# Which queue carries the opening loads: strict order on SyncE, a table load first and two weight blocks on ScalarE

## The chip, the cores and the metric

One core of one Trainium2 chip. The metric is the device time of one launch in microseconds (us). TensorE is written PE, VectorE DVE, ScalarE ACT, GpSimd POOL and SyncE SP. "Landed" is when a transfer's completion semaphore is full. One program on one core has no second die to compare with.

## The reference, cut to what matters

```python
x = A_x                                   # 2048 x 640, bf16
xn = layernorm(x)
q, k, v = split(xn @ wqkv)                # 32 heads of 20
pq, pk = q @ w_phi, k @ w_phi             # per head
phi = concat(softmax(p), softmax(-p))     # feature map, for q and k
kv, z = sum over s of phi_k (x) v, phi_k
o = phi_q kv / (phi_q z + 1e-6)
return x + o @ wo + (silu(xn @ w1) * (xn @ w3)) @ w2
```

The opening concerns only the first 512 rows (four tiles of 128 rows, called rows 0 to 3 below), their normalisation, and v = xn @ wv for them. The matrix wv is loaded in five blocks of 128 x 640 (160 KB), and a row tile has 160 KB too.

## The kernel before

The loads of the opening, as issued:

```python
def load_wv(c, queue=nc.sync):
    queue.dma_start(out=wv[:, c, :], in_=wqkv3[:, c, 2 * D : 3 * D])

def setup():
    ...
    nc.vector.memset(xg[0][:, 0, 320:328], 0.0)
    nc.sync.dma_start(out=xg[0][:, 0, 0:320], in_=x2[0:P, 0:320])        # row 0, first half
    nc.scalar.dma_start(out=xg[0][:, 0, 320:640], in_=x2[0:P, 320:640])  # row 0, second half
    load_x(xg[0], 1, 1, 0)          # row 1
    load_wv(0, nc.scalar)
    load_wv(1)
    load_wv(2, nc.scalar)
    load_x(xg[0], 2, 1, 0)          # row 2
    load_wv(3, nc.scalar)
    load_wv(4)
    load_x(xg[0], 3, 1, 0)          # row 3
    load_gu(0)                      # first gate/up weights: 2 x 480 KB
    ...                             # wrow, load_gu(1), wkT (transposed), rows 4-7, load_gu(2), load_gu(3)

def warm():
    warm_ps.append(bank([P, 512], f32))
    dummies(8)                      # 8 matmuls of 512 columns on constants, the first work of TensorE
```

What uses them, in the order in which TensorE and VectorE take it (cut):

```python
plan.op("ACT", 1.3, lambda: nc.scalar.preload_act_table(AF.Sqrt), after=3.2)
ln_stats(0); c0 = center(0, 0, 256); ...          # VectorE: row 0
x0 = [T(0, ...)(), T(0, ...)()]                   # TensorE: transposes of row 0
ln_stats(1); c2 = center(1, 0, 640)
V_part(0, (0, 1), ...); V_part(0, (2,), ...)      # v of row 0, wv blocks 0, 1, 2
e2, e3 = T(1, ...)                                # transposes of row 1
vo[0]["last"] = V_part(0, (3, 4), ...)            # v of row 0, wv blocks 3, 4
...
ln_stats(2); ...; apply2 = ln_apply(2)
V_part(1, (0, 1), ...); V_part(1, (2, 3, 4), ...) # v of row 1, all five blocks
e2, e3 = T(2, ..., apply2)                        # transposes of row 2
...                                               # v of rows 2 and 3, then gate/up matmuls without pause
```

The softmax here doesn't subtract the row's maximum and nothing guards it: scores larger than these inputs give would overflow.

## Time and profile before

| | before |
|---|---|
| time | 269.59 us (median of 6; 269.18 to 270.17) |
| span of the profiled execution | 267.9 us |
| first gate/up matmul ("dense start" below) | 13.38 us |

From the page of the kernel before: span, busy time by engine, DMA queues (q1 is SyncE's, q10 ScalarE's: packets, MB, share of 16 engines), and the engines of the chain of work that ended last.

```profile
span 267.9 us, 5109 instructions
...
PE 262.6 (98%) x1948; PEld 165.1 (62%) x1974; DVE 173.8 (65%) x334; ACT 122.4 (46%) x273; POOL 131.5 (49%) x118
...
q1 hardware_dynamic: 68784, 37.18, 50.8%
q10 hardware_dynamic: 720, 0.61, 0.7%
...
PE 96%; DMA 2%; issue 1%; ACTq 0%; DVE 0%
```

The chain is TensorE nearly throughout. From 13.4 us on its gaps sum to 1.4 us. So a change to the opening can gain only by moving the moment at which this dense work starts.

TensorE's timeline of the kernel before, 3 to 15 us. Columns: start us, length us, engine, line, operation, out<-in, shape, count, and in brackets idle time ahead with what ended it.

```profile
4.21 0.73 PE L416 MATMUL bank<-ident,xn 128*128 128x128 bf16 x5
...
5.08 1.60 PE L461 MATMUL bank<-wv,xnT 128*128 128x320 bf16 x6
...
7.14 2.08 PE L461 MATMUL bank<-wv,xnT 128*128 128x320 bf16 x14 [0.17 <-DMA wv<-in_A_wqkv_dram]
9.12 0.73 PE L416 MATMUL bank<-ident,xn 128*128 128x128 bf16 x10
...
13.38 1.24 PE L667 MATMUL bank<-xnT,w_107 128*128 128x512 bf16 x4
```

L416 are the transposes, L461 the v matmuls, L667 gate/up. Six v matmuls take 1.60 us at 5.08 but fourteen take 2.08 us at 7.14: the same shape at half the rate, then at full rate.

VectorE's timeline of the kernel before: row 2's statistics and, 1.7 us later, its normalised tile.

```profile
6.92 0.89 DVE L297 BATCH_NORM_STATS2 stats<-xg 128x6 f32<-128x320 bf16 x2 [0.90 <-DMA xg<-in_A_x_dram]
...
8.61 0.45 DVE L352 TENSOR_SCALAR xn<-xg,mv,rstd 128x640 bf16<-128x640 bf16 x1
```

VectorE was idle for 0.90 us until row 2 landed (6.89 us); its tile is done at 9.06, and TensorE takes it at 9.12.

ScalarE's timeline of the kernel before, 0 to 6 us. ACTq is its sequencer issuing transfers.

```profile
0.96 0.38 ACTq L183 DMA_DIRECT2D xg<-in_A_x_dram  x1
1.36 1.42 ACTq L175 DMA_DIRECT2D wv<-in_A_wqkv_dram  x3
2.82 1.28 ACT L915 ACT_TABLE_LOAD   x1 [2.82 <-issue]
```

The windows 2:4, 4:6 and 6:8 us of the kernel before. The last two columns are the mean busy share of the DMA engines and GB/s.

```profile
2.00:4.00 2.00, 2.00 (x6) 0.59 (x4) 1.23 (x4) 1.18 (x1) 1.25 (x10) 1.00 0.99 280
4.00:6.00 2.00, 2.00 (x13) 1.27 (x13) 1.92 (x7) 1.20 (x4) 0.00 (x0) 1.00 1.03 309
6.00:8.00 2.00, 1.83 (x16) 1.19 (x15) 1.06 (x5) 0.75 (x2) 0.00 (x0) 1.00 1.00 305
```

The DMA engines are full all through the opening.

### The profile page before, as it was taken

The numbers are of one execution on the slowest core, as the hardware profiler recorded it, in microseconds if no ns is written. First come the engines' busy times: TensorE is split into PE (matmuls) and PEld (weight loads), VectorE is DVE, ScalarE is ACT, GpSimd is POOL, SyncE is SP. The second block draws the span as 40 slices with busy tenths as digits, with TensorE's granted clock in tenths as the row PEclk, the third lists the DMA queues.
The fourth block names the chain that finished last, engine by engine and source line by source line (L and its number), as shares of the span: only waits on it lengthen the run. The fifth ranks groups of instructions, "written<-read, shape, count | busy, mean of one in ns | idle before, by whom it ended". The sixth has DMA issues, their size and how long they took to land.

```text
span 267.9 us, 5109 instructions
## 1 busy us (share of the span) xinstructions
PE 262.6 (98%) x1948; PEld 165.1 (62%) x1974; DVE 173.8 (65%) x334; ACT 122.4 (46%) x273; POOL 131.5 (49%) x118
## 2 busy tenths in 40 slices
PE   8999999999999999999999999999999999999995
PEld 4645555555565666666555677765765665657774
DVE  4738798777665996876898748666367365443221
ACT  3857676656776676767545222234225213120000
POOL 3263679976557577699315715443542553111000
PEclk9999999999999999999999999999999999999999
DMA  7999949200420027529295457495913938430401
GB/s 210 310 264 300 265 128 298 74 0 0 134 64 0 2 98 202 115 108 148 77 292 179 130 144 201 150 258 183 220 38 119 234 112 210 123 82 20 124 25 49
DMA packets 69528, 38.10 MB, mean 142 GB/s; under 512 B 49664, under 2 KB 67456, under 8 KB 69504
## 3 DMA queue, kind: packets, MB, share of 16 engines
q1 hardware_dynamic: 68784, 37.18, 50.8%
q10 hardware_dynamic: 720, 0.61, 0.7%
q8 instruction: 15, 0.25, 0.4%
q14 instruction: 9, 0.07, 0.1%
HBM read 12.81 MB, written 12.98 MB: 96 GB/s over the span
## 4 chain that ended last, share of the span: by engine, by line
PE 96%; DMA 2%; issue 1%; ACTq 0%; DVE 0%
PE bank L667 38%; PE bank L447 22%; PE bank L832 19%; PE bank L845 8%; PE rtbank L742 2%; PE bank L461 2%; DMA wv<-in_A_wqkv_dram 2%; PE bank L620 1%; PE kva L592 1%; PE kvb L592 1%; PE bank L416 0%; ACTq L175 0%; ACTq L183 0%; DVE res L859 0%; DVE xg L181 0%
## 5 line engine op out<-in xcount | busy, mean ns | idle before, releaser
L711 POOL TENSOR_TENSOR hT<-gs,up 128x512 bf16<-128x512 bf16 x43 | 49.7, 1156 | 81.0 <-ACT up L706 41.8
L667 PE MATMUL bank<-xnT,w_108 128*128 128x512 bf16 x235 | 59.2, 379 | 0.3
L667 PE MATMUL bank<-xnT,w_107 128*128 128x512 bf16 x219 | 58.2, 379 | 1.1
L832 PE MATMUL bank<-w_109,hT 128*128 128x320 bf16 (+2 forms) x396 | 55.1, 295 | 0.0
L447 PEld LDWEIGHTS <-xnT 128*128 128x128 bf16 x440 | 42.1, 98 | 17.6
L832 PEld LDWEIGHTS <-hT 128*128 128x128 bf16 x396 | 37.9, 98 | 15.2
L683 ACT ACTIVATE th<-bank 128x512 bf16<-128x512 f32 x48 | 28.7, 597 | 39.8 <-PE bank L667 39.1
L688 DVE SCALAR_TENSOR_TENSOR gs<-th,bank 128x512 bf16<-128x512 bf16 x48 | 32.8, 684 | 20.6 <-ACT th L683 20.0
L667 PEld LDWEIGHTS <-w_108 128*128 128x128 bf16 x240 | 23.5, 98 | 28.3
L859 DVE TENSOR_TENSOR res<-bank,xr 128x320 bf16<-128x320 f32 (+2 forms) x33 | 15.8, 478 | 38.6 <-PE bank L845 38.6
L706 ACT ACTIVATE up<-bank 128x512 bf16<-128x512 f32 x43 | 25.7, 597 | 22.5 <-PE bank L667 22.5
L667 PEld LDWEIGHTS <-w_107 128*128 128x128 bf16 x240 | 22.4, 97 | 20.9
L845 PE MATMUL bank<-wo,oT 128*128 128x320 bf16 (+2 forms) x165 | 24.7, 295 | 0.0
L447 PE MATMUL bank<-wkphi,xnT 128*128 128x320 bf16 x160 | 24.3, 299 | 0.0
L447 PE MATMUL bank<-wqphi,xnT 128*128 128x320 bf16 x160 | 24.3, 299 | 0.0
L845 PEld LDWEIGHTS <-oT 128*128 128x128 bf16 x165 | 15.8, 98 | 5.8
L447 PE MATMUL bank<-wv,xnT 128*128 128x320 bf16 x120 | 18.3, 299 | 0.0
L519 ACT ACTIVATE exp_128<-bank 128x320 bf16<-128x320 f32 x32 | 11.5, 435 | 13.6 <-PE bank L447 13.6
L519 ACT ACTIVATE exp_131<-bank 128x320 bf16<-128x320 f32 x32 | 11.5, 437 | 12.2 <-PE bank L447 12.2
L519 ACT ACTIVATE exp_129<-bank 128x320 bf16<-128x320 f32 x32 | 11.5, 435 | 10.7 <-PE bank L447 10.7
L519 ACT ACTIVATE exp_130<-bank 128x320 bf16<-128x320 f32 x32 | 11.5, 439 | 10.1 <-PE bank L447 10.1
L297 DVE BATCH_NORM_STATS2 stats<-xg 128x6 f32<-128x320 bf16 x32 | 13.7, 470 | 2.7 <-DMA xg<-in_A_x_dram 2.7
(141 smaller groups left out, 294.5 us busy)
## 6 DMA issues: line engine op xcount, KB each, us to landing
xr<-in_A_x_dram SPq DMA_DIRECT2D x4, 640.0 KB, 5.4
out_dram<-res SPq DMA_DIRECT2D x15, 160.0 KB, 1.9
w_107<-in_B_w_dram SPq DMA_DIRECT2D x4, 480.0 KB, 6.5
w_108<-in_B_w_dram SPq DMA_DIRECT2D x4, 480.0 KB, 6.8
w_109<-in_B_w_dram SPq DMA_DIRECT2D x1, 1920.0 KB, 8.7
xg<-in_A_x_dram SPq DMA_DIRECT2D x11, 160.0 KB, 3.7
wo<-in_A_wo_dram SPq DMA_DIRECT2D x1, 800.0 KB, 5.1
xg<-in_A_x_dram SPq DMA_DIRECT2D x1, 640.0 KB, 5.1
```

Source lines behind the costliest of these rows:

```text
L297: nc.vector.bn_stats(out=stats[:, t, h, :], in_=xg[c][:, i, h * 320 : (h + 1) * 320])
L447: nc.tensor.matmul(o["ps"][:], xnT[:, c, t * P : (t + 1) * P], w[:, c, 320 * half : 320 * half + 320], start=(c == 0), stop=(c == KD - 1),)
L461: nc.tensor.matmul(o[half]["ps"][:], xnT[:, c, t * P : (t + 1) * P], wv[:, c, 320 * half : 320 * half + 320], start=(c == 0), stop=(c == K ...
L519: nc.scalar.activation(out=box["e"][:, sgn, 16 * half : 16 * half + 16, :], in_=o["ps"][:].rearrange("p (h d) -> p h d", d=Dh), func=AF.Ex ...
L667: nc.tensor.matmul(o["ps"][:], w[:, k, fi * P : (fi + 1) * P], xs[:, k, :], start=(k == 0), stop=(k == KD - 1))
L683: nc.scalar.activation(out=box["th"][:], in_=og["ps"][:], func=AF.Tanh, scale=0.5)
L688: nc.vector.scalar_tensor_tensor(out=box["gs"][:], in0=box["th"][:], scalar=1.0, in1=og["ps"][:], op0=ALU.add, op1=ALU.mult)
L706: nc.scalar.activation(out=box["up"][:], in_=ou["ps"][:], func=AF.Copy, scale=0.5)
L711: lambda: nc.gpsimd.tensor_mul(out=hT[c][:, fi, :], in0=box["gs"][:], in1=box["up"][:]),
L832: nc.tensor.matmul(o["ps"][:], hT[c][:, fi, ti * P : (ti + 1) * P], w2[:, fi, lo:hi], start=(fi == 0), stop=False,)
L845: nc.tensor.matmul(o["ps"][:], oT[c][:, k, ti * P : (ti + 1) * P], wo_of[0][:, k, lo:hi], start=False, stop=(k == KD - 1),)
L859: nc.vector.tensor_tensor(out=box["res"][:, lo:hi], in0=o["ps"][:], in1=xr[c][:, ti, lo:hi], op=ALU.add)
```

## The change

Its intent: land the opening tiles in the order of their use by sending them down one queue, get the activation table out of the way first, and let ScalarE carry only two blocks that are used late. Rows 8 to 13 are also loaded in pairs.

```diff
         nc.vector.memset(xg[0][:, 0, 320:328], 0.0)
+        nc.scalar.preload_act_table(AF.Sqrt)
         nc.sync.dma_start(out=xg[0][:, 0, 0:320], in_=x2[0:P, 0:320])
-        nc.scalar.dma_start(out=xg[0][:, 0, 320:640], in_=x2[0:P, 320:640])
+        nc.sync.dma_start(out=xg[0][:, 0, 320:640], in_=x2[0:P, 320:640])
         load_x(xg[0], 1, 1, 0)
-        load_wv(0, nc.scalar)
+        load_wv(0)
         load_wv(1)
-        load_wv(2, nc.scalar)
+        load_wv(2)
+        load_wv(3, nc.scalar)
         load_x(xg[0], 2, 1, 0)
-        load_wv(3, nc.scalar)
-        load_wv(4)
+        load_wv(4, nc.scalar)
         load_x(xg[0], 3, 1, 0)
 ...
-        X_of[t] = plan.op("SP", 0.5, lambda: [load_x(xg[c], i, 1, c)], ...)
+        n = 2 if t < 14 else 1
+        if i % n == 0:
+            X_of[t] = plan.op("SP", 0.5, lambda: [load_x(xg[c], i, n, c)], ...)
+        else:
+            X_of[t] = X_of[t - 1]
 ...
-    plan.op("ACT", 1.3, lambda: nc.scalar.preload_act_table(AF.Sqrt), after=3.2)
```

More of the change, by code (lines that the diff above doesn't have):

```diff
@@ L403, in fetch @@
             xg_of[c] = plan.alloc("five", al)
-        X_of[t] = plan.op("SP", 0.5, lambda: [load_x(xg[c], i, 1, c)], deps=[xg_of[c]], lat=2.5, after=30.0)
+        n = 2 if t < 14 else 1
+        if i % n == 0:
+            X_of[t] = plan.op("SP", 0.5, lambda: [load_x(xg[c], i, n, c)], deps=[xg_of[c]], lat=2.5, after=30.0)
+        else:
+            X_of[t] = X_of[t - 1]
         ln_stats(t, ("k", k))
```

## The prediction

> **What bounds the kernel now.** TensorE. The page gives PE 98% busy; the chain that ended last is 96% PE. After 13.4 us the PE idle gaps in the trace sum to only 1.4 us of 254, none over 0.06 us, so nothing changed there can gain. The one DMA piece on the chain is in the opening: 4.77 us for a wv load that ended at 7.10 us. So the question is when the dense gate/up work (13.38 us on the timeline) can start.
>
> **The opening before.** x and wv are nine 160 KB blocks (one split in halves), issued on two queues, about 0.46 us an issue. They land: row 0 at 2.68/2.89, row 1 3.81, wv0 4.99, wv1 5.21, wv2 5.57, row 2 6.89, wv3 7.10, wv4 7.39, row 3 7.82. The DMA engines are full from 2 to 14 us (DMA share about 1.0, 270 to 325 GB/s). The page total is fixed, so the change can only reorder. TensorE then is never far from its feeder: it idles about 0.2 to 0.3 us for wv3 at 7.14; row 2's transposes at 9.12 follow VectorE's normalised row (9.06), which follows the landing of row 2 (VectorE idled 0.90 us for it, timeline); small waits for ScalarE/VectorE copies at 9.87 and 11.9.
>
> **What the change does.**
> 1. Takes three issues and half of row 0 from ScalarE to SyncE. Row 0's second half is issued 0.3 us later (1.25 instead of 0.96) but shares less; I expect it at about 2.9 to 3.1. First statistics and transposes: within 0.15 us of before.
> 2. The table load (1.28 us, at 2.82 before, followed by 0.56 us of ScalarE idle) was off the chain. Moving it gains nothing directly.
> 3. The Trainium skill, "Perfetto Trace Analysis", "DVE / Act Engine Instruction", says that the sequencer pushes an instruction and goes on to decode the next. The trace agrees for VectorE (a semaphore instruction at 2.92 inside a statistics instruction of 2.71 to 3.20). So I expect wv3's issue by 1.0 us, beside the table load, not behind it (65%); otherwise at 2.1. wv4 waits for a recycled semaphore (row 0's first half, about 2.7). So "late" blocks come early and share bandwidth with rows 0, 1 and wv0/wv1: wv3 lands near 4.0, wv4 near 6.0, wv1 5.2 to 5.9, wv2 5.5 to 6.2, row 2 6.6 to 7.2, row 3 7.2 to 7.8. (Estimate: the slowest engine's rate, 1.47 MB by 7.82 us, some 0.27 MB/us.)
> 4. The wv3 wait of 0.3 us goes, but wv1/wv2 may cost TensorE some of it, and row 2's chain moves by -0.3 to +0.3 us.
> 5. Rows 8 to 13 in pairs: eight issues become five. They were at 27 to 31 us on SyncE; no VectorE wait for them shows, and the transposed group 1 lands at 42.7 while its first use is at 49.5. No effect. The planner's order of VectorE/ScalarE work may shift slightly, within slack.
>
> **Sum.** Opening ends -0.5 to +0.3 us from before, best -0.15; the rest carries it unchanged. Predicted 269.4 us, 8 in 10 between 268.6 and 270.1. Faster by over 2%: 0.01; within 2%: 0.985; slower: 0.005.
>
> **What would show it.** Right: PE busy time unchanged; first gate/up matmul at 12.9 to 13.7; no wait for wv3/wv4; the time difference equals the shift of that matmul; wkT still lands near 18.7 before its use. Wrong on 3: wv3's issue after the table load's end. Wrong on 5: a PE or VectorE wait over 0.3 us after 25 us.
>
> **What would make it wrong.** Strict order letting row 2 land before 6.5 (gain to 1 us); a planner reorder starving TensorE; another moment of the clock's warm-up (matmuls were slow until 6.5 us).

## The result, and the profile after

| | before | after |
|---|---|---|
| median of the same rounds | 269.44 us (20 runs) | 270.14 us (10 runs; 269.75 to 271.06) |
| ratio of the fast runs | | 1.0031, 95% interval 1.0019 to 1.0044 |
| profiled execution | 269.57 us | 271.37 us |
| first gate/up matmul | 13.38 us | 13.99 us |

A ratio is the mean time of one kernel's fast runs over that of the other's fast runs of the same rounds, so it is not quite the ratio of the medians. The change is a small loss, some 0.8 us. The runs of the changed kernel fall in two clusters, six at 269.75 to 270.32 and four at 270.77 to 271.06. The profiled execution is slower than any of them, so it must not be taken for a typical one.

When each opening transfer landed, in us, worked out from the completion records of the two traces:

```
          row0a row0b row1  wv0   wv1   wv2   row2  wv3   wv4   row3  w1[0]  w3[0]  wkT    rows4-7
before    2.68  2.89  3.81  4.99  5.21  5.57  6.89  7.10  7.39  7.82   9.56  11.32  18.70  20.31
after     3.21  3.90  5.62  6.04  6.46  7.10  7.51  3.38  4.19  7.90  12.02  13.45  20.74  23.38
```

From the page of the changed kernel:

```profile
span 269.7 us, 5106 instructions
...
PE 262.5 (97%) x1948; PEld 164.6 (61%) x1974; DVE 173.9 (64%) x334; ACT 122.5 (45%) x273; POOL 131.6 (49%) x118
...
q1 hardware_dynamic: 69024, 37.42, 50.8%
q10 hardware_dynamic: 432, 0.36, 0.4%
...
PE 89%; SPq 5%; DMA 3%; issue 1%; DVE 1%
```

TensorE does the same work in the same busy time, but transfers and SyncE's issuing now take 8% of the chain, where transfers took 2% before. ScalarE's timeline of the changed kernel shows what its two "late" blocks did:

```profile
0.79 1.28 ACT L182 ACT_TABLE_LOAD   x1 [0.79 <-PEq L1098]
0.82 0.87 ACTq L175 DMA_DIRECT2D wv<-in_A_wqkv_dram  x2
```

They are issued at 0.82 and 1.24 us, beside the table load and before SyncE's second transfer. They land first of all weights (3.38 and 4.19). VectorE's timeline of the changed kernel: rows 0, 1 and 2 are waited for in turn.

```profile
3.23 0.49 DVE L298 BATCH_NORM_STATS2 stats<-xg 128x6 f32<-128x320 bf16 x1 [2.30 <-DMA xg<-in_A_x_dram]
4.00 0.49 DVE L298 BATCH_NORM_STATS2 stats<-xg 128x6 f32<-128x320 bf16 x1 [0.28 <-DMA xg<-in_A_x_dram]
...
7.54 0.89 DVE L298 BATCH_NORM_STATS2 stats<-xg 128x6 f32<-128x320 bf16 x2 [0.17 <-DMA xg<-in_A_x_dram]
...
9.23 0.45 DVE L353 TENSOR_SCALAR xn<-xg,mv,rstd 128x640 bf16<-128x640 bf16 x1
```

TensorE's timeline of the changed kernel:

```profile
5.12 0.57 PE L421 MATMUL bank<-ident,xn 128*128 128x128 bf16 x5 [0.71 <-DVE xn L343]
...
6.08 0.85 PE L466 MATMUL bank<-wv,xnT 128*128 128x320 bf16 x4 [0.22 <-DMA wv<-in_A_wqkv_dram]
...
9.73 0.73 PE L421 MATMUL bank<-ident,xn 128*128 128x128 bf16 x10
...
13.99 1.24 PE L672 MATMUL bank<-xnT,w_107 128*128 128x512 bf16 x4
```

Row 0's transposes come 0.9 us later than before, and there is now a gap of 0.71 us behind the warm-up matmuls. By the dense start the delay is 0.61 us, and row 2's landing is 0.62 us later (7.51 against 6.89). From row 2's landing to its transposes both kernels take 2.2 us, from there to the dense start both take 4.26 us (13.38 - 9.12 and 13.99 - 9.73).

After the dense start this execution loses another 1.2 us (271.37 - 13.99 is 257.38; in the kernel before 269.57 - 13.38 is 256.19). TensorE's waits of the changed kernel from 12 to 30 us (the kernel before has none there):

```profile
PE bank L625 <- DVE gs L693: 0.9, 1, 0.9
PE bank L625 <- DMA wkT<-in_A_wqkv_dram: 0.2, 1, 0.2
```

The weights come later, and the issue of the first gate/up load waits longer. SyncE's waits in the first 30 us, first of the kernel before, then of the changed kernel. Columns: issuing line, what it waited for, us in total, times, longest.

```profile
SPq L172 <- DMA wv<-in_A_wqkv_dram: 0.8, 1, 0.8
```

```profile
SPq L172 <- DMA xg<-in_A_x_dram: 1.1, 1, 1.1
```

The program has eight completion semaphores for these transfers, used in turn; the trace shows the ninth transfer and later ones waiting until the earlier user of their semaphore has landed. In the changed kernel the first gate/up load waits for row 1 (5.62), and is issued at 5.63 instead of 3.83. The windows 2:4, 4:6, 6:8 of the changed kernel show a hole in the transfers from 6 us on:

```profile
2.00:4.00 2.00, 2.00 (x6) 0.59 (x4) 0.49 (x1) 0.07 (x1) 1.26 (x10) 1.00 0.97 293
4.00:6.00 2.00, 1.15 (x9) 0.55 (x9) 1.58 (x5) 0.56 (x2) 0.00 (x0) 1.00 0.97 309
6.00:8.00 2.00, 1.71 (x14) 1.08 (x14) 1.75 (x7) 0.77 (x4) 0.00 (x0) 1.00 0.76 203
```

The late issue alone does not make the weights this late. e17 below issues the first gate/up load at 5.61 us and has as deep a hole (215 GB/s from 6 to 8 us), and its wkT lands at 19.32, 0.6 us later than in the kernel before and not 2.0. e5 issues it at 5.28, and wkT lands at 18.82. What held this execution's weights up beyond that stays open.

### The profile page after: what moved, and what is told of

It reads as the page before. It is cut to its first block, busy times and chain, and to the rows that moved or that the text cites. A ratio compares the mean times of both kernels' runs of the same rounds, so it can differ in the third digit from the quotient of the medians.

```text
span 269.7 us, 5106 instructions
## 1 busy us (share of the span) xinstructions
PE 262.5 (97%) x1948; PEld 164.6 (61%) x1974; DVE 173.9 (64%) x334; ACT 122.5 (45%) x273; POOL 131.6 (49%) x118
## 4 chain that ended last, share of the span: by engine, by line
PE 89%; SPq 5%; DMA 3%; issue 1%; DVE 1%
PE bank L672 35%; PE bank L452 22%; PE bank L837 19%; PE bank L850 8%; DMA xg<-in_A_x_dram 3%; SPq L196 3%; PE rtbank L747 2%; SPq L172 2%; PE kva L597 1%; PE kvb L597 1%; PE bank L625 1%; DVE stats L298 0%; DVE gs L693 0%; SPq L194 0%; SPq L184 0%
```

## The experiments

Theory A at the start: ScalarE's two blocks, issued too early, starve row 0. Rival B: SyncE's queue has too much to issue. Rival C: the paired loads. Rival D: the moved table load. All ratios are against the kernel before in the same rounds.

### e1 to e4: hold the two blocks, take them away from ScalarE, undo the pairs, move the table alone

e1, the changed kernel with

```diff
+        nc.scalar.copy(out=wv[:, 3, 0:8], in_=nc.const_aps.tensor(1.0, [P, 8], bf))
         load_wv(3, nc.scalar)
```

> The changed kernel, with one tiny ScalarE copy into wv block 3 after the table load, so that ScalarE's two late blocks really wait for the table (issue at about 2.4 us instead of 0.82). Theory A (ScalarE's two blocks, issued beside the table load, took bandwidth from row 0): row 0 lands by 2.7 and 3.1 us, row 1 by 4.2, the first gate/up matmul comes by 13.4 instead of 13.99, time 269.2 to 269.6 us. Rival B (SyncE's queue is simply too long: three issues of 0.46 us moved onto it): row 0 and 1 stay late, time stays at 269.9 to 270.3.

Measured: 270.00 us (before 269.71), ratio 1.0014 (1.0001 to 1.0027). Row 0 landed at 2.68 and 3.29, row 1 at 4.18, as theory A had it, and yet row 2 came at 7.81, wv block 2 at 7.37 and the dense start at 14.28. So row 0 was starved by the early blocks, but giving it back did not bring the dense start back. The loss is about half of the changed kernel's (1.0014 against 1.0031), but the two intervals overlap. Theory A names a true effect that does not decide the time alone.

e2, the changed kernel with

```diff
-        load_wv(3, nc.scalar)
+        load_wv(3)
-        load_wv(4, nc.scalar)
+        load_wv(4)
```

> The changed kernel with wv blocks 3 and 4 on SyncE too, at the same places of the program: no transfer on ScalarE at the opening. Theory A: row 0 lands at about 2.5 and 2.9 us, the first gate/up matmul by 13.3, time at or under that of before (268.9 to 269.5). Rival B: SyncE's queue is longest here, five issues more than before, so the opening ends later than in the changed kernel, time 270.3 or more.

Measured: 271.08 us (before 269.71), ratio 1.0057 (1.0035 to 1.0079), the slowest but one of all. Row 0 at 2.62 and 3.63, wv block 4 only at 8.65, and TensorE waits for it. Strict order on one queue alone is worse still than the change. This went as rival B said, and theory A as I had put it fell.

e3, the changed kernel with

```diff
-        n = 2 if t < 14 else 1
+        n = 1
```

> The changed kernel with rows 8 to 15 loaded one by one again, as before. Theory A: nothing changes, 269.9 to 270.4 us, opening as in the changed kernel (row 0 at 3.2 and 3.9). Rival C (the paired loads cost the time): back to 269.4.

Measured: 269.97 us (before 269.71), ratio 1.0018 (1.0003 to 1.0033). The interval overlaps with that of the changed kernel (1.0019 to 1.0044), the opening is the same (row 0 at 3.36 and 3.90). The pairs are not the cause; e12 below, single rows too, is no faster than e7 and e17 with pairs. The profile of e3, the slowest of its six runs (270.93 us), brought the second lead. TensorE's timeline of e3:

```profile
5.12 0.73 PE L421 MATMUL bank<-ident,xn 128*128 128x128 bf16 x5 [0.72 <-DVE xn L343]
...
6.27 1.76 PE L466 MATMUL bank<-wv,xnT 128*128 128x320 bf16 x6
...
8.35 2.26 PE L466 MATMUL bank<-wv,xnT 128*128 128x320 bf16 x14
10.46 0.72 PE L421 MATMUL bank<-ident,xn 128*128 128x128 bf16 x10
```

Six v matmuls take 1.76 us, in the first profile of the changed kernel six took 0.85 + 0.43. In e3 the single matmuls start 0.27 us apart up to 8.6 us, and 0.135 us apart from then on. Row 2 landed at 7.56, but its transposes came at 10.46 (2.9 us later, not 2.2), because TensorE itself was late. The Trainium skill ("TensorE: Matmul & The Clock Gate", "Part 1: The HAM clock gate") says that TensorE starts at half its rate and goes to the full one after being busy through a window of some 3.4 us, whose phase is not the kernel's. The trace agrees with the two rates (matmuls 0.27 and 0.135 us apart); the window itself is not seen in it. In the kernel before, whose TensorE has no gap until 6.9 us, the rate rose at about 6.4; here, with a gap of 0.72 us behind the warm-up, at 8.6. Sixteen traces hold a clock event for the rise: it lies between 3.61 us (e8) and 6.74 us (e17). A gap does not always put it off: the changed kernel's first profile (gap 0.71 us) and e16 (0.78 us) were at the full rate at their first transposes, at 5.1 us.

e4, the kernel before with the table load ahead of ScalarE's transfers, as in the change:

```diff
+        nc.scalar.preload_act_table(AF.Sqrt)
         nc.sync.dma_start(out=xg[0][:, 0, 0:320], in_=x2[0:P, 0:320])
 ...
-    plan.op("ACT", 1.3, lambda: nc.scalar.preload_act_table(AF.Sqrt), after=3.2)
```

> The kernel before with only the table load moved ahead of ScalarE's four transfers. Theory A: the sequencer issues the transfers beside the table load, so landings are those of before within 0.1 us, time as before, 269.2 to 269.6. Rival D (the table load holds ScalarE's transfers up, or its move costs): transfers start at 2.1 us, row 0's second half lands near 4, time 270.5 or more.

Measured: 270.27 us (before 269.71), ratio 1.0030 (0.9999 to 1.0061), spread 269.45 to 272.74: unclear. The table load holds nothing up (row 0's second half is issued at 0.95, beside it). But the order of the semaphores changed with it. ScalarE's timeline of e4:

```profile
0.79 1.28 ACT L182 ACT_TABLE_LOAD   x1 [0.79 <-PEq L1094]
...
1.36 3.44 ACTq L175 DMA_DIRECT2D wv<-in_A_wqkv_dram  x3
```

Three issues now stretch over 3.44 us instead of 1.42: wv block 3 reuses row 1's semaphore and is issued at 4.47, when row 1 has landed. It lands at 7.35, TensorE waits 0.7 us for it, although row 2 came early (6.13). So moving an instruction that costs nothing itself moved a load by two microseconds through the reuse of semaphores.

### e5: row 2's place alone

The traces so far suggested theory E: the dense start is 6.49 us after row 2's landing, or about 6 us after the last wv block if that is later, whatever rows 0 and 1 do.

```diff
-        load_x(xg[0], 2, 1, 0)
         load_wv(3, nc.scalar)
         load_wv(4)
+        load_x(xg[0], 2, 1, 0)
```

> The kernel before with one line moved: row 2's load stands behind wv block 4 on SyncE, so it lands eighth or ninth instead of seventh; rows 0 and 1 are untouched. Theory E (the dense part starts 6.49 us after row 2 lands, or about 6.0 us after the last wv block, whatever rows 0 and 1 do; read from the traces of before, after and e1): row 2 lands at 7.3 to 7.6, first gate/up matmul at 13.8 to 14.1, time up by 0.3 to 0.7 us. Rival A (row 0's late landing was the loss): nothing changes, 269.4 to 269.7.

Measured: 269.80 us (before 269.49), ratio 1.0004 (0.9988 to 1.0020). In the profiled execution row 2 landed at 7.48, as late as in the changed kernel, with row 0 on time (2.62 and 2.83), and the dense start was at 13.96; both are as expected. The timed runs lean the same way (+0.3 us in the median) but their interval includes no change. It ends at 0.54 us, a little under the 0.59 us by which row 2 was late in the profiled execution (the slowest of the six), so the time does not confirm theory E; that execution's trace does.

### e6 and e9: row 0 late, and more warm-up

e6, the kernel before with

```diff
+        load_wv(0, nc.scalar)
         nc.scalar.dma_start(out=xg[0][:, 0, 320:640], in_=x2[0:P, 320:640])
         load_x(xg[0], 1, 1, 0)
-        load_wv(0, nc.scalar)
```

> The kernel before with ScalarE's first two transfers swapped: wv block 0 ahead of row 0's second half, which then lands at 3.6 to 4.2 us instead of 2.89, as in the changed kernel; row 2 and the last wv blocks keep their places. Theory E: first gate/up matmul within 0.3 us of 13.4 where the PE clock rises by 6.7 us; executions where it rises late may lose 0.7. Rival A: up by 0.6 us or more in every execution, first gate/up matmul at 14.0 or later.

Measured: 270.95 us median of five fast runs, ratio 1.0043 (1.0024 to 1.0063): one at 269.92 and four at 270.89 to 271.21. The profiled execution, slow, took 563.57 us. It is no time to compare with. From the page of e6:

```profile
PE 550.8 (98%) x1948; PEld 256.5 (46%) x1974; DVE 171.3 (30%) x334; ACT 127.0 (23%) x273; POOL 131.4 (23%) x118
...
L667 PE MATMUL bank<-xnT,w 128*128 128x512 bf16 x454 | 225.1, 681 | 6.3 <-issue 6.3
```

The gate/up matmul takes 681 ns on average instead of 379, TensorE is 98% busy, and its rate never rises in 550 us. The trace has a gap of 0.76 us behind the warm-up matmuls, but the gap did not cause this: the warm-up matmuls, which run before it, are already as slow as the gate/up matmuls later. Matmuls of 512 columns, ns min/median/max and first and last start in us: the warm-up and the gate/up of e6, then the warm-up of e9, which has the same loads:

```profile
L227 PE MATMUL bank<-const-bfloat16-1.0 x8: 587/722/723, 0.8 to 4.0; 128*128 128x512 bf16 x8
L667 PE MATMUL bank<-xnT,w x454: 586/722/723, 20.8 to 508.0; 128*128 128x512 bf16 x152
L227 PE MATMUL bank<-const-bfloat16-1.0 x11: 381/631/631, 0.8 to 4.5; 128*128 128x512 bf16 x11
```

In the other traces the warm-up matmuls start 427 ns apart before the rise, in this one 443 or 559 ns. So this execution was slow from its first matmuls on, and why stays open. Its granted clock reads 1.000, but its trace holds no clock event at all, so that figure measures nothing here.

e9 is e6 with `dummies(11)` instead of `dummies(8)`.

> e6 (row 0 late, 4 of 5 runs near 271.0, one stuck at half clock) with 11 warm-up matmuls instead of 8, so that TensorE does not idle from 4.4 to 5.1 us. Theory F (with row 0 late, TensorE idles between the warm-up and the first transposes, and the clock then rises late or never in most executions): every run at 269.5 to 270.3, none near 271 and none over 300, clock at full rate by 6 us. If the runs stay near 271, it is row 0's landing itself that costs (rival A), and F is wrong.

Measured: 269.76 us (before 269.58), ratio 1.0014 (1.0000 to 1.0027), all five runs at 269.63 to 270.28. TensorE's timeline of e9: the late row 0 is still there. The rate is full from 4.0 us, where the last warm-up matmuls start 0.22 us apart.

```profile
5.38 0.57 PE L416 MATMUL bank<-ident,xn 128*128 128x128 bf16 x5 [0.52 <-DVE xn L342]
...
6.13 0.99 PE L461 MATMUL bank<-wv,xnT 128*128 128x320 bf16 x6
...
13.53 1.67 PE L667 MATMUL bank<-xnT,w 128*128 128x512 bf16 x6
```

Row 0 lands as late as in e6 (3.21 and 4.16 here, 3.27 and 4.18 there), so some 0.8 us of e6's loss (1.0043 less 1.0014) was not row 0's landing: it goes with three fewer warm-up matmuls. Theory F (a gap behind the warm-up lets the rate rise late, or never) passes this test in its first half, but none of e6's four runs near 271 us was traced. "Or never" is not shown, since the one stuck execution was slow before its gap. More warm-up did not close the gap altogether: at full rate the eleven matmuls are done sooner.

### e7, e12, e16 and e17: the same for the changed kernel

e7 and e17 are the changed kernel with `dummies(11)`, e12 is e3 with it, e16 is the changed kernel as it is.

> The changed kernel with 11 warm-up matmuls instead of 8, so that TensorE is not idle from 4.4 to 5.1 us. Theory F (the executions at 270.8 to 271.1 are those where the PE clock rose only at about 8.7 us, as in the profile of e3): no run above 270.4, median 269.8 to 270.1, the clock at full rate by 6 us. If the slow cluster stays, F is wrong and its cause lies elsewhere, for instance in late weights.

> e3 (the changed kernel with single row loads, whose profile showed the clock rising only at 8.7 us) with 11 warm-up matmuls, a second sample for theory F beside e7: no run above 270.5, where e3 and the changed kernel had about one in three at 270.7 to 271.1; median 269.8 to 270.1, so that 0.4 us or so of the loss stays.

> The changed kernel once more, for the spread of its runs on one chip beside e17: one to two of five runs at 270.7 or more, the others near 269.9, if the two clusters of its first ten runs are real.

> e7 once more, on the same chip as e16. Theory F for the changed kernel: no run at 270.7 or more, mean 0.2 to 0.5 us under that of e16. If the means agree within 0.15 us and the slow runs come here too, the clock's rise is not what makes the changed kernel's slow cluster.

| | warm-up | ratio (95%) | runs at 270.5 us or more |
|---|---|---|---|
| first result | 8 | 1.0031 (1.0019 to 1.0044) | 4 of 10 |
| e3 | 8 | 1.0018 (1.0003 to 1.0033) | 1 of 6 |
| e16 | 8 | 1.0044 (1.0026 to 1.0061) | 4 of 6 |
| e7 | 11 | 1.0017 (1.0001 to 1.0033) | 0 of 5 |
| e12 | 11 | 1.0027 (1.0013 to 1.0040) | 1 of 5 |
| e17 | 11 | 1.0023 (1.0011 to 1.0036) | 0 of 5 |

e12's run at 270.94 went against its expectation. The first row leaves out its profiled execution (271.37); the others count theirs. Together it is 9 of 22 runs with eight warm-up matmuls and 1 of 15 with eleven. On one chip, e16 against e17, the means are 270.57 and 269.99 us: 0.58 us of the loss goes with three more matmuls that do nothing, more than the 0.2 to 0.5 expected (the intervals of their ratios still overlap). What stays with eleven is 1.0017 to 1.0027, some 0.5 to 0.7 us. The kernel before with eleven was not run; with eight, none of its runs is over 270.33.

### e8: late weights alone

The kernel before; the first gate/up load and all SyncE loads behind it are issued only once VectorE has centred row 1, by way of a small memset of w1 that they overwrite.

```diff
-        load_gu(0)
+    def weights():
+        nc.vector.memset(w1[:, 0, 0:8], 0.0)
+        load_gu(0)
 ...            # and in center(): after the instruction for t == 1, weights()
```

> The kernel before with all gate/up weight loads and what follows them on SyncE held until VectorE has centred row 1 (about 5.9 us, against 3.83 before and 5.63 in the changed kernel), the opening otherwise the same. Theory G (late weights are a second loss of their own): wkT lands at 20 to 21 us, TensorE waits for it or for group 1's statistics between 19.8 and 26 us by 0.3 to 1.5 us, time up by as much, with the first gate/up matmul at or before 13.4. If the time stays at 269.4 to 269.7, late weights cost nothing.

Measured: 269.50 us (before 269.49), ratio 1.0003 (0.9985 to 1.0021). The first load was issued at 6.76, wkT landed at 20.07. In the profiled execution (270.07 us) the dense start was early (13.29), and TensorE then waited 0.19 us for wkT and 0.12 us for the statistics of rows 4 to 7. But the other runs were mostly as before (269.32 to 269.61, and one 270.51). So late weights can cost some tenths, and go with 1.2 us in the first profile of the changed kernel, but not in the typical run. In five traces whose dense start was late itself (e2, e3, e12, e16, e17) there is no such wait: wkT lands at 19.32 to 20.71 us there, and a later dense start needs it later.

### e10: row 2 moved up in the changed kernel

```diff
         load_x(xg[0], 1, 1, 0)
+        load_x(xg[0], 2, 1, 0)
         load_wv(0)
 ...
-        load_x(xg[0], 2, 1, 0)
```

> The changed kernel with row 2's load moved up behind row 1's, ahead of wv 0 to 2. Theory E in its full form (the dense part needs row 2 and all five wv blocks, 1.3 MB in whatever order): row 2 lands near 6 us but wv block 2 at 7.3 to 7.7, first gate/up matmul at 13.9 to 14.5, no gain over the changed kernel: 269.8 to 270.9. Rival H (only row 2's rank was at fault): row 2 at 6 us brings the first gate/up matmul to 13.3 or less and the time to 269.5 or less.

Measured: 271.53 us (before 269.58), ratio 1.0069 (1.0056 to 1.0082), the worst of all. Row 2 landed at 6.08, but wv block 0 at 6.52 and block 2 at 7.43, TensorE was idle 0.61 us behind the warm-up and 0.80 us more for wv, and the dense start was at 14.17. Rival H is refuted: moving row 2 forward on SyncE's queue takes from the weights what it gives. The time was higher than expected. Its TensorE gaps are among the longest, which would fit theory F, but that was not tested here. Three of its five runs (271.53 to 271.78) list a granted clock of 0.994, as does e4's slowest (272.74), where other runs list 0.998 to 1.000; that was not followed up.

### e11, e13 and e14: fewer bytes, two queues, fewer issues

All three give a wrong result on purpose (relative error 0.36): wv blocks 3 and 4 are zeroed by VectorE and never loaded. e11 is the changed kernel with

```diff
-        load_wv(3, nc.scalar)
+        nc.vector.memset(wv[:, 3:5, :], 0.0)
-        load_wv(4, nc.scalar)
```

> A wrong result on purpose: the changed kernel without its two ScalarE transfers, wv blocks 3 and 4 being zeroed by VectorE instead, so 0.33 MB fewer bytes in the opening. Theory E (bytes ahead of row 2 and the last wv block set the opening; SyncE's issue rate does not): row 0 by 2.7 and 3.2, row 2 at 6.0 to 6.6, first gate/up matmul at 12.5 to 13.1, time 268.5 to 269.2. Rival B (the length of SyncE's queue sets it): row 2 stays at 7.2 or later and time at 269.8 or more.

e13 is e11 with row 0's second half and wv blocks 0 and 2 on ScalarE. e14 is e11 with wv blocks 0 to 2 in one load on SyncE.

> Wrong result on purpose, as e11 (wv 3 and 4 zeroed, not loaded): the same eight transfers, but row 0's second half and wv 0 and 2 go through ScalarE. Theory J (one queue alone leaves the DMA engines partly idle, two keep them full, so splitting the opening over both is what the kernel before had and the changed one gave up): DMA share 2 to 7 us near 1.0 instead of 0.76 to 0.92, row 2 lands by 6.2 instead of 7.08, first gate/up matmul at 12.3 to 13.0, time 268.5 to 269.2. If row 2 still lands at 7 or later, J is wrong and the bytes or HBM set the pace.

> Wrong result on purpose, as e11, but wv 0 to 2 come in one load on SyncE instead of three: two issues of 0.46 us fewer ahead of row 2, still one queue. If SyncE's issue rate sets the pace: row 2 lands 0.5 us or more sooner than in e11 (by 6.6), time 269.2 or less. If it is the single queue's draining (J): row 2 at 6.8 to 7.3 still, time as e11, 269.5 to 269.9.

| | queues, issues ahead of row 2 on SyncE | row 2 landed | dense start | time (before) |
|---|---|---|---|---|
| e11 | one, 6 | 7.08 | 13.55 | 269.67 (269.58) |
| e13 | two, 3 | 5.99 | 13.12 | 269.23 (269.12) |
| e14 | one, 4 | 6.68 | 13.54 | 269.83 (269.12) |

The window 2 to 7 us, first of e11, then of e13:

```profile
2.00:7.00 5.00, 4.48 (x21) 2.06 (x20) 3.27 (x10) 1.18 (x4) 1.26 (x10) 1.00 0.85 232
```

```profile
2.00:7.00 5.00, 5.00 (x26) 2.43 (x25) 3.95 (x12) 1.18 (x4) 1.24 (x10) 1.00 0.97 292
```

Two of nine blocks less to load in the opening bought little on one queue: row 2 came 0.3 us earlier than the 7.39 us that it takes on average with the changed kernel's loads, and not at 6.0 to 6.6 as expected. The DMA engines moved 232 GB/s, 85% busy. With the same eight transfers on two queues they moved 292 GB/s (some gate/up weights among them, issued from 3.14 instead of 4.55 us) and brought row 2 in 1.09 us earlier. Theory E's half about bytes alone fell with e11.

Two things differ between e11 and e13, the number of queues and the times of issue: row 2 was issued at 3.60 in e11, at 2.67 in e14 and at 2.18 in e13. e14, with two issues fewer on one queue, brought 0.40 us of the 1.09, and its 6.68 lies between what its two theories had said (by 6.6; 6.8 to 7.3). So issue time is part of it; how much a second queue gives beyond issuing sooner was not separated. In e11's trace three transfers behind the first land 2.42 to 2.47 us after their issue, the next three 3.44 to 3.48 us and row 3 4.09 us: the lateness is not made good. A few packets in both traces take 300 to 1,190 ns instead of 55. That a second queue fills the engines in such moments is an inference; the traces do not tell the packets' engines apart.

And e13 shows the floor: with all loads early, TensorE has no wait left and the dense start is still at 13.12. Against 13.38 before, by these two traces no order of loads gains more than some 0.3 us unless TensorE's own opening work or its slow rate changes. The ratio of e13 is 1.0001 (0.9988 to 1.0013), of e11 1.0008 (0.9995 to 1.0020), of e14, whose TensorE waits 1.07 us for the joint load, 1.0029 (1.0015 to 1.0043).

### e15: a candidate

The kernel before with wv blocks 3 and 4 as one load on ScalarE.

```diff
-        load_wv(3, nc.scalar)
-        load_wv(4)
+        nc.scalar.dma_start(out=wv[:, 3:5, :], in_=wqkv3[:, 3:5, 2 * D : 3 * D])
```

> A candidate to beat both: the kernel before with wv 3 and 4 as one load of 320 KB on ScalarE, so nine transfers before the gate/up weights and one recycled-semaphore wait fewer. Row 2 at 6.5 to 6.9, wv 3 and 4 together at 7.0 to 7.4, first gate/up matmul 13.1 to 13.5, time 269.1 to 269.7: at best 0.2 us better than before.

Measured: 270.54 us (before 269.12), ratio 1.0048 (1.0035 to 1.0060). Row 2 landed at 6.68 as expected, but the joint load only at 7.60, row 1 at 5.35, and TensorE waited for weights twice (0.27 and 0.21 us). It is a loss, and why most of its runs are at 270.2 to 270.7 was not followed up. No version here beats the kernel before.

### What the executions have in common

Dense start less row 2's landing, from all traces in which row 2 came last:

```
               before after  e1     e5     e7     e11    e12    e16    e17
row 2 landed    6.89   7.51   7.81   7.48   7.20   7.08   7.20   7.57   7.28
dense start    13.38  13.99  14.28  13.96  13.68  13.55  13.68  14.05  13.78
difference      6.49   6.48   6.47   6.48   6.48   6.47   6.48   6.48   6.50
```

Where it is larger, another thing came last: the last wv block (e2, e4, e10, e14, e15), or TensorE's slow rate or its own work (e3, e6, e8, e9, e13). And the time less the dense start is 256.0 to 256.3 us in every execution without a later wait of TensorE (before 256.19, e1 255.98, e2 256.04, e16 255.99).

## Why the prediction was wrong

It gave 269.4 us with 268.6 to 270.1, and 270.14 was measured: right on "within 2%", just outside its range, and wrong in sign against the kernel before.

- **What bounds the kernel: right.** PE busy time is unchanged (262.6 and 262.5 us), and where TensorE has no later wait the loss is the shift of the dense start: the rigid 256 us behind it held in fourteen executions. That matmul was expected at 12.9 to 13.7 us and came at 13.99.
- **Step 1 (row 0 within 0.15 us): wrong.** Row 0 landed at 3.21 and 3.90 and its transposes came 0.91 us later. Step 3 had the early issue right (wv3 at 0.82, beside the table load, as the Trainium skill's "Perfetto Trace Analysis", "DVE / Act Engine Instruction", let one expect), but step 1 did not draw the conclusion that both blocks would then run ahead of row 0. It also had wv4 waiting for a recycled semaphore; it was issued at 1.24.
- **Step 2 (the table load's move gains nothing directly): right, with a side effect unseen.** In e4 it reordered the semaphores and held a load for two microseconds.
- **Step 4 (row 2's chain between -0.3 and +0.3 us, from step 3's landing at 6.6 to 7.2): the mis-sized term, and the step that failed.** Row 2's landing moved by +0.62 us in the profile, to 7.51. Over the profiles with the changed kernel's loads (after, e3, e7, e12, e16, e17) it is 7.39 us on average, over those with the load split of before and row 2 ahead of the last blocks (before, e6, e8, e9, e15) 6.85. (e4, whose semaphores fell in another order, is left out; with it the second is 6.73.) That 0.54 us matches what stays of the loss with more warm-up (0.5 to 0.7 us). I computed with total bytes at one rate; the place in the order (e5) matters, and so does how the loads are split over two queues (1.09 us, e11 against e13), be it by earlier issue or by draining.
- **"wkT still lands near 18.7": wrong.** 20.74 in the profile. The first gate/up load waited for row 1's semaphore, but in e17 it waited as long and wkT came at 19.32, so the rest is open. wkT and the statistics behind it made TensorE wait 1.08 us in that execution, but little in a typical one (e8).
- **The clock: named among the dangers, given no weight.** It is the other half. Row 0's lateness opens a gap of 0.7 us behind the warm-up matmuls, and the slow cluster nearly vanishes with three more of them (e16 and e17, and most clearly e6 and e9). This is shown as an effect of the warm-up on the times; that the rate rises late, at 8.6 us, is seen in the trace of e3 only.
- **Step 5 (pairs without effect): right** (e3, e12). Its own sign of an error, a wait of over 0.3 us after 25 us, did show (TensorE's 0.93 us, ended at 25.15), but that wait belongs to rows 4 to 7, which are not loaded in pairs.

Open: why the changed kernel's first profile lost 1.2 us behind the dense start while e16's lost nothing there (in the first, packets of the transposed load took 1.49 us at 16.6 us, just beside a fetch of 16 KB of instructions; nothing was tried on that), what makes single packets slow, what slowed e6's 563.57 us execution from its start, and e15.

## What to carry to other kernels

Here two queues issuing the opening's loads kept the DMA engines fuller than one queue in perfect order (292 against 232 GB/s, e13 and e11), so an order of use is better tried by interleaving two queues than by giving one up. A transfer put behind other work on ScalarE was late only where it waited for a semaphore (0.82 us beside the table load, 2.31 behind e1's copy). Find the one tile from whose landing the dense part is a fixed distance away, and judge a reorder by that tile, not by the first one. Cover the wait for the first tile with warm-up work up to the first real matmul: with a gap of 0.7 us there the times fell into two clusters, and a change that delays the first tile needs its warm-up sized again.

## What the Trainium skill lacked or had wrong

- "DMA: Bandwidth & Descriptors", "Issuing engines are not separate DMA queues": it says that issuing from several engines "will only save the time on the sequencer it takes to initiate the DMA, which is usually small relative to the DMA itself". Here the DMA engines moved 232 GB/s in the window 2 to 7 us with the opening's eight transfers on one queue and 292 GB/s with them on two, and a tile landed 1.09 us earlier (e11, e13). Merging three issues into one on the single queue brought 0.40 us of it (e14), so issue time was not small; whether it was all was not separated.
- "TensorE: Matmul & The Clock Gate", Part 1: the page gives the window of some 3.4 us and warns of stuck states, but does not tell what a short gap in the warm-up does: with one of 0.72 us behind 3.6 us of warm-up the rate rose at 8.6 us (e3), with as long a gap in two other traces by 5.1. Nor, beyond the stuck states, does it tell of an execution slow from its first matmul to its last (563.57 us, warm-up matmuls 722 ns instead of 631, gate/up 681 instead of 379, e6).
- The same page warns that clock-gate trace events can be unreliable and advises a second metric; it does not say that a mean granted clock can read 1.000 because no event was recorded at all (563.57 us, e6). The spacing of matmuls shows the rate (starts 443 or 559 ns apart instead of 216).
- No page tells what a limited set of completion semaphores used in turn does to later issues: an unrelated instruction moved (e4) and a load was issued at 4.47 instead of 2.33 us.
